# Three 512-column score units per key tile in six shared PSUM banks, and projections issued as 64-column pairs

## The chip, the cores and the metric

The kernel runs on one core of a Trainium2 chip. The metric is the device time of one execution in microseconds (us). Engines are named as the profile names them: PE is TensorE's matrix multiply, PEld its weight load, DVE is VectorE, ACT is ScalarE, POOL is GpSimd, SP is SyncE, which here only issues DMAs. PSUM is the memory that PE writes; it has eight banks, each of 512 float32 columns over 128 partitions.

## The reference

Two stages follow each other. First a routed attention over 4 batches and 8 heads, 768 positions, head size 64: a query sees only the keys whose nearest centroid (16 a head) is its own. Then a gated long convolution over the positions, with the attention's output as input (512 channels).

```python
q_assign = np.argmax(np.einsum('bhsd,hcd->bhsc', q_n, c_n), axis=-1)
k_assign = np.argmax(np.einsum('bhsd,hcd->bhsc', k_n, c_n), axis=-1)
mask = q_assign[:, :, :, None] == k_assign[:, :, None, :]
scores = np.where(mask, scale * np.matmul(q, k.transpose(0, 1, 3, 2)), -1000000000.0)
attn = softmax(scores)            # over the keys
x = np.matmul(attn, v)            # heads side by side: (4, 768, 512)
...
x1, x2, x3 = split(x @ w_proj)    # three times 512 columns
x2_conv = irfft(rfft(x2, axis=1) * rfft(filter_fft, axis=0), axis=1)
out = (x1 * x2_conv * x3) @ w_out
```

## The kernel before

Nothing is looped at run time. `build` writes down a list of operations, each with the engines that can do it, an estimated duration, a due time and what it reads and writes; `Plan.place` then puts them one by one on the engine that can start one first, among those about equally early the one with the earliest due time. The sequence that comes out is emitted as the program, so each engine runs a fixed list in order and waits where a needed result is late.

The attention works in 8 groups `n` of four heads (half a batch), each in two pairs `pr` of heads; a pair has six key tiles `sk` of 128 keys, so there are 96 key tiles. The operations that the change and the prediction speak of, with the lines of the kernel before:

- `tr` (L474): transposes of q and k, three 128x128 float32 transposes to one PSUM bank, copied out to `qkT` (L230 on ACT, L232 on DVE) and cast to `aug` (bfloat16, with 16 rows of one-hot cluster marks, `ohT`, below or above them, which makes the mask part of the product).
- `sim` (L494), `simT` (L505), `ohT` (L531): products with the centroids, their transposes, and the transposes of the one-hot marks; between them DVE finds the maxima (L509 to L521).
- `score` (L56, through `columns`): for one key tile and one head, four matmuls with 64 weight columns each into a pair of PSUM banks, 2 x 384 queries; `columns` issues two such matmuls, one for each half of the output's partitions, in the place of one with 128 weight columns.
- `exp` (L564): ACT reads the pair of banks (128 x 768) and writes the probabilities to `p`, of which there are four buffers (`NPB`), each for a key tile of both heads.
- `pv` (L575): the product with v for both heads, four float32 matmuls (each runs as two passes, so eight rows in the trace), accumulated over the six key tiles in banks 4 and 5; `acc` (L586) sums the probabilities on DVE; `den` (L599) adds them over the partitions.
- the convolution of a batch, spread between later attention work: `U` (L688), `spectrum` (L388, L392), `G` (L733), `I` (L758), `W` (L780). All but L392 are issued with 128 weight columns. The filter's own spectrum is computed once near the start with the same `spectrum`, from `filter_fft`, which DVE first adds and subtracts to `uv2` (L362).

PE is set to a tile shape by each matmul: 128 weight columns (projections, transposes), 64 (`score`, `pv`, `columns`), or 32 (`sim`, `den`), on 128 rows, and 64 rows x 128 columns for half of `I`. Two matmuls with 64 columns on different halves run beside each other. The planner charges 0.1 us for a change of shape (`switch`).

PSUM before: banks 0 to 3 are two pairs for scores alone, 4 and 5 the accumulator of `pv`, and 6 and 7 take everything else ("fill"); `banks_for` decides this. Before the first and after the last score the reserved banks are open to others too.

Queues: SP issues the loads of q, k, v, of `filter_fft` and the masks' rows; POOL's queue issues the loads of `w_proj` (`wpj`, needed first by `U`) and `w_out`.

Of the kernel before, what the change touches and what calls it, by code (L numbers as in the profile page):

```python
# [30 lines left out]
NPB = 4  # L31
# [3 lines left out]
MODES = {"pv": 64, "score": 64, "bc": 64, "sim": 32, "den": 32}  # L35
# [24 lines left out]
class Plan:  # L60
# [33 lines left out]
    def place(self, free0, banks_for, switch=0.1, wait=0.1, rate=215e3, bonus=4.0):  # L94
# [4 lines left out]
        st = SimpleNamespace(pool=0.0, dve=0.0, bw=0.0, last=None, kind=None, score=0, o=0, tail=0)  # L99
# [13 lines left out]
        while n < len(self.ops):  # L113
            best = None
            for e, lst in ready.items():
# [14 lines left out]
                if not cand:  # L130
# [3 lines left out]
                    c[1].due - (bonus if e == "PE" and st.kind == "pv" == c[1].kind else 0.0)  # L134
                    + (c[0] - t0) * 20, c[1].seq))
# [5 lines left out]
            if o.alloc is not None:  # L141
# [5 lines left out]
                if o.alloc.cls not in ("score", "o"):  # L147
                    st.tail |= (st.score == st.scores and min(o.alloc.ids) < 4) + 2 * (
                        st.o == st.otiles and any(i in (4, 5) for i in o.alloc.ids))
            d = o.eng[e]  # L150
            if e == "PE":
                mode = MODES.get(o.kind, 128)
                if mode != st.last:
                    d += switch
                st.last, st.kind = mode, o.kind
            o.start, o.on = t, e
            free[e] = t + d
            busy[e] += d
            o.end = t + d
# [8 lines left out]
            for h in o.free:  # L168
                h.readers -= 1
                h.end = max(h.end, o.end)  # L170
                if not h.readers:
                    for i in h.ids:
                        bank_free[i] = h.end + 0.06
# [12 lines left out]
def banks_for(bank, free, st, o):  # L186
# [5 lines left out]
    if bank.cls == "score":  # L192
        two = min(((0, 1), (2, 3)), key=lambda p: max(free[p[0]], free[p[1]]))
        t = max(free[two[0]], free[two[1]]) if st.score else whole(0, 4)
        return (two, t) if t < 1e8 else None
# [3 lines left out]
    allowed, first = [6, 7], []  # L199
    if st.score == 0:  # L200
        allowed += [0, 1, 2, 3] if bank.cls == "head" else []
    elif st.score == st.scores:
        if st.tail & 1:
            allowed += [0, 1, 2, 3]
        elif whole(0, 4) < 1e8:
            first += [0, 1, 2, 3]
    if st.o == 0:
        allowed += [4, 5] if bank.cls == "head" else []
    elif st.o == st.otiles:
        if st.tail & 2:  # L210
            allowed += [4, 5]
        elif whole(4, 6) < 1e8:
            first += [4, 5]
    t = lambda i: whole(*((0, 4) if i < 4 else (4, 6))) if i in first else free[i]
# [4 lines left out]
def build(T):  # L219
# [14 lines left out]
    columns = lambda *a: halves(T.nc.tensor)(*a)  # L234
# [10 lines left out]
    def two(h):  # L245
        return T.pair[h.ids[0] // 2]
# [770 lines left out]
```

## Time and profile before

| | before |
|---|---|
| median of 3 runs | 443.53 us (443.04 to 444.03) |
| the profiled execution | 443.23 us |
| its span, first to last instruction | 441.4 us |
| PE busy | 409.6 us, 93% |
| DVE busy | 355.5 us, 81% |
| ACT busy | 268.8 us, 61% |
| POOL busy | 96.0 us, 22% |
| granted PE clock, mean | 0.994 |

A busy PE is not a measure of its work here: the end of a matmul is modelled and lies behind the start of the next one. What an operation holds PE for is read from the start of its first matmul to the start of the next operation's first one.

### The profile page before, as it was taken

To read this page: it belongs to the slowest core of one execution; us is meant where nothing else is said; L and a number is where in the kernel's file an instruction comes from. 1 tells how busy PE (TensorE), PEld (TensorE's weight loads), DVE (VectorE), ACT (ScalarE), POOL (GpSimd) and SP (SyncE) were. 2 spreads that over 40 slices of the span, in tenths; PEclk is the share of its full clock that TensorE was granted. 3 is DMA by queue.
4 is the path that set the end of the run, shared out by engine and by line. 5 is a ranking of instruction groups with operands and counts; after the bars stand their busy time and mean duration, and the time that the engine had idled before them with its cause. 6 is when DMAs were issued, how large, how long until landed. Compare 5 with 4: busy or idle time off the path is not lost.

```text
span 441.4 us, 7484 instructions
## 1 busy us (share of the span) xinstructions
PE 409.6 (93%) x2824; PEld 189.8 (43%) x2840; DVE 355.5 (81%) x486; ACT 268.8 (61%) x411; POOL 96.0 (22%) x94
## 2 busy tenths in 40 slices
PE   4987698999999999999999999998999989999994
PEld 3444244444444444343434444443443434444541
DVE  7984999799897978687768977998956987887962
ACT  5885356688675566566574676757674455655242
POOL 6420000002102762111100541302300531220330
PEclk9999899999999999999999999999999999999999
DMA  9969806244421133112561114211140100111023
GB/s 198 169 128 251 182 20 146 73 107 97 106 74 49 43 74 93 53 47 81 193 135 36 55 38 107 73 44 48 61 156 5 52 1 1 38 38 50 1 95 143
DMA packets 67356, 37.11 MB, mean 84 GB/s; under 512 B 56764, under 2 KB 62456, under 8 KB 67320
## 3 DMA queue, kind: packets, MB, share of 16 engines
q1 hardware_dynamic: 62856, 33.62, 29.0%
q0 software_dynamic: 1056, 2.10, 2.7%
q10 hardware_dynamic: 3408, 0.92, 1.1%
q8 instruction: 22, 0.36, 0.3%
q14 instruction: 14, 0.11, 0.1%
HBM read 30.66 MB, written 6.48 MB: 84 GB/s over the span
## 4 chain that ended last, share of the span: by engine, by line
PE 66%; DVE 15%; DMA 7%; ACT 5%; issue 4%; SPq 1%; POOL 1%; ACTq 1%; DVEq 0%; POOLq 0%
PE pair L575 19%; PE pair L56 10%; PE bank L733 10%; DVE acc L586 6%; PE bank L688 5%; PE bank L780 5%; PE bank L758 4%; DMA y<-in_moe_filter_fft_dram 4%; PE bank L474 3%; PE bank L388 3%; PE bank L599 2%; DVE osb L648 2%; ACT p L564 2%; DVE uT L659 2%; PE bank L494 2%
## 5 line engine op out<-in xcount | busy, mean ns | idle before, releaser
L564 ACT ACTIVATE p<-pair 128x768 f32<-128x768 f32 x192 | 148.2, 811 | 65.8 <-PE pair L56 51.3
L575 PE MATMUL pair<-p,vraw 128*64 128x385 f32 x768 | 140.1, 493 | 0.9 <-ACT osb L591 0.9
L586 DVE TENSOR_TENSOR acc<-acc,p 128x1536 f32<-128x1536 f32 x64 | 116.7, 1823 | 5.9 <-ACT p L564 3.9
L56 PE MATMUL pair<-aug,aug 80*64 80x384 bf16 (+1 forms) x768 | 88.1, 334 | 6.9 <-ACT p L564 6.5
L575 PEld LDWEIGHTS pair<-p,vraw 128*64 128x64 f32 x768 | 56.1, 137 | 52.2 <-issue 43.1
L56 PEld LDWEIGHTS <-aug 80*64 80x64 bf16 (+1 forms) x768 | 37.9, 109 | 54.6 <-issue 46.1
L710 POOL TENSOR_TENSOR y<-tm 128x512 bf16<-128x512 f32 x21 | 36.1, 1729 | 113.0 <-DVE tm L706 84.3
L733 PE MATMUL bank<-xT,wpj 128*128 128x384 bf16 x256 | 48.2, 327 | 0.4 <-ACT qkT L230 0.4
L768 POOL TENSOR_TENSOR y<-yy,x 128x768 bf16<-128x768 f32 x12 | 25.2, 2100 | 98.4 <-DVE yy L764 73.2
L232 POOL CAST aug<-qkT 64x768 bf16<-64x768 f32 x18 | 20.6, 1144 | 112.8 <-ACT qkT L230 105.3
L474 PE MATMUL bank<-ident,qkraw 128*128 128x128 f32 x192 | 34.1, 301 | 8.3 <-DMA qkraw<-in_q_dram 5.2
L733 PEld LDWEIGHTS <-wpj 128*128 128x128 bf16 x256 | 22.5, 98 | 26.9 <-issue 14.9
L474 PEld LDWEIGHTS bank<-ident,qkraw 128*128 128x128 f32 x192 | 22.5, 149 | 24.8 <-issue 6.5
L230 ACT COPY qkT<-bank 128x384 f32<-128x384 f32 x50 | 23.0, 484 | 16.1 <-PE bank L733 8.8
L706 DVE TENSOR_TENSOR tm<-bank,hm 128x512 f32<-128x512 f32 x48 | 30.2, 681 | 2.0 <-PE bank L388 1.9
L586 DVE TENSOR_TENSOR acc<-p,p 128x1536 f32<-128x1536 f32 x16 | 28.5, 1781 | 3.2 <-PE bank L599 2.6
L688 PE MATMUL bank<-wpj,uT 128*128 128x512 bf16 x91 | 22.3, 380 | 0.9 <-DVE den L232 0.5
L780 PE MATMUL bank<-wout,y 128*128 128x512 bf16 x90 | 21.9, 380 | 0.4 <-POOL y L768 0.2
L232 DVE COPY qkT<-bank 128x384 f32<-128x384 f32 x22 | 12.1, 552 | 11.5 <-PE bank L474 11.2
L742 DVE TENSOR_TENSOR x<-bank,x 128x384 f32<-128x384 f32 x24 | 13.3, 552 | 9.6 <-PE bank L733 9.2
L230 ACT CAST aug<-qkT 64x768 bf16<-64x768 f32 x24 | 19.9, 829 | 0.8 <-DVE qkT L232 0.4
L758 PE MATMUL bank<-inv,y 128*128 128x384 bf16 (+1 forms) x128 | 20.0, 328 | 0.0
(136 smaller groups left out, 394.3 us busy)
## 6 DMA issues: line engine op xcount, KB each, us to landing
vraw<-in_v_dram SPq DMA_DIRECT2D x16, 384.0 KB
qkraw<-in_q_dram SPq DMA_DIRECT2D x30, 192.0 KB
qkraw<-in_k_dram SPq DMA_DIRECT2D x30, 192.0 KB
rb<-dr SPq DMA_DIRECT2D x30, 192.0 KB
out_dram<-ob SPq DMA_DIRECT2D x11, 512.0 KB
wpj<-in_moe_w_proj_dram POOLq DMA_DIRECT2D x1, 1536.0 KB, 13.6
y<-in_moe_filter_fft_dram SPq DMA_DIRECT2D x4, 384.0 KB
aug<-ohT SPq DMA_DIRECT2D x60, 24.0 KB
```

Source lines behind the costliest of these rows:

```text
L56: tensor.matmul(out[64 * i:64 * i + 64], lhsT[:, 64 * i:64 * i + 64], rhs, start=start, stop=stop)
L230: T.nc.scalar.copy(out, in_)
L232: (T.nc.vector if e == "DVE" else T.nc.gpsimd).tensor_copy(out, in_)
L474: T.nc.tensor.transpose(ap(h)[:, ts(t, 128)], T.qkraw[s][:, 3 * ch + t].rearrange("p h d -> p (h d)"), T.ident)
L564: ex = op(("ACT", .82 + (1.28 if first[0] is None else 0)), lambda e, h=h, s=s, hp=hp: T.nc.scalar.activation(T.p[s][:, hp, :S].rearrange( ...
L575: T.nc.tensor.matmul(o[64 * hp:64 * hp + 64, ch, :385], T.vraw[vs][:, hp, sk * D:(sk + 1) * D], T.p[slots[sk]][:, hp, 384 * ch:384 * ch + ...
L586: T.nc.vector.tensor_tensor(T.acc[:], x, T.p[slots[sk]][:, :, :S], op=Alu.add)
L688: T.nc.tensor.matmul(ap(h), f[:, e_, kt, ts(m, 128)], T.wpj[:, kt, DM:2 * DM], start=(kt == 0), stop=(kt == ND - 1))
L710: op(({"POOL": 1.45, "DVE": .68} if i < 2 else {"DVE": .68}) if last else ("POOL", 1.45), lambda e, i=i, r=r: alu(e).tensor_tensor(T.y[:, ...
L733: T.nc.tensor.matmul(ap(h)[:, :384], T.wpj[:, kt, off + dt * 128:off + dt * 128 + 128], T.xT[xs][:, kt, ts(ch, 384)], start=(kt == 0), sto ...
L758: T.nc.tensor.matmul(bk(hh, e_)[:, :384], T.y[lo:hi, i, cs, ts(dt, 128)], T.inv[lo:hi, row], start=(n == 0), stop=(n == 3))
L780: T.nc.tensor.matmul(ap(h), T.y2[:, kt, ts(2 * tt + e_, 128)], T.wout[:, kt], start=(kt == 0), stop=(kt == ND - 1))
```

## The change

**Banks.** Banks 0 to 3, 6 and 7 become six single banks for scores and fill alike. While scores are running, `banks_for` gives neither class more than `HELD` = 4 of them. Only 4 and 5 keep their special role.

**Scores.** The two heads' scores of a key tile, 2 x 768 columns, are cut into three units of 512 columns, each in one bank (`THIRDS`): 512 of the first head, 256 of each, 512 of the second. A unit is one `score` operation and one `exp`, so a key tile has three of each, where it had two. The middle unit has four pairs' halves of 256 columns.

**Shapes.** `U`, `spectrum`, `G`, `W`, the transposes `ohT` and half of `I` go through `columns` (or its like): two matmuls with 64 weight columns in the place of one with 128. The float32 transposes `tr`, `simT` stay at 128 columns, `sim` and `den` at 32. From the third group on, the transposes of both halves of a q or k tile (`tr2`, six of them, two banks) are one operation, and so are both halves of `sim` and of `simT`.

**Planner.** `place` adds 1.5 us (`shape`) to the due time of a PE operation that would change the shape, counts 0.16 us from PE's end to a result (`AFTER`), and 0.09 and 0.08 us of overlap on ACT and DVE (`OVERLAP`).

**Small things.** Three DVE operations on the one-hot marks are issued once for both halves (128 x 768) where there were two each. POOL copies one element of the filter's buffer into `wpj` ahead of the load of `w_proj`, so this load starts only after `filter_fft` has landed; the load of `w_out` stands ahead of it.

On PE, where the first convolution's `G` begins to mix with the attention (`bank` numbers are buffers, `pair` is the score's two banks, `wpj` the weights of `G`, `aug` those of the score). Before:

```order
L733 LDWEIGHTS wpj
L733 MATMUL bank_64<-xT_136,wpj 128x384
L599 MATMUL bank_63<-acc,ones_67 32x384 x4
L474 MATMUL bank_64<-ident,qkraw_87 128x128 x3
L56 LDWEIGHTS aug_103
L56 MATMUL pair_438<-aug_102,aug_103 64x384
```

The same place in the changed program, where L62 is `columns`, L476 `tr2` and L597 `pv`:

```order
L62 LDWEIGHTS aug_109
L62 MATMUL bank_65<-aug_108,aug_109 64x512
L597 MATMUL pair_492<-p_117,vraw_97 64x385 x4
L476 MATMUL bank_63<-ident,qkraw_91 128x128 x3
L476 MATMUL bank_66<-ident,qkraw_91 128x128 x3
L62 LDWEIGHTS wpj
L62 MATMUL bank_67<-xT_140,wpj 64x384
```

Before, the output's first number tells four shapes in six rows (128, 32, 128, 64 columns), three changes; now score, `pv` and `G` all have 64, and the two changes that are left stand around six transposes. Over the whole program the shape changes 284 times before and 134 times now.

On DVE, near the start, where the filter's `uv` (L362, now L363) stands among the first pair's sums `acc` (L586, now L608). Before:

```order
L516 TENSOR_TENSOR oh<-oh,revc 128x384
L519 TENSOR_REDUCE m_86<-oh 128x24
L521 TENSOR_TENSOR oh<-oh,m_86 128x384
L586 TENSOR_TENSOR acc<-acc,p_112 128x1536
L362 TENSOR_TENSOR uv_139<-y,y_141 128x1536 x2
L586 TENSOR_TENSOR acc<-acc,p_113 128x1536
L586 TENSOR_TENSOR acc<-acc,p_110 128x1536
```

Now:

```order
L608 TENSOR_TENSOR acc<-p_114,p_115 128x1536
L608 TENSOR_TENSOR acc<-acc,p_116 128x1536
L608 TENSOR_TENSOR acc<-acc,p_117 128x1536
L233 COPY sim<-bank_66 128x384
L608 TENSOR_TENSOR acc<-acc,p_114 128x1536
L608 TENSOR_TENSOR acc<-acc,p_115 128x1536
L363 TENSOR_TENSOR uv_143<-y,y_145 128x1536 x2
```

All five sums of the first pair now stand ahead of `uv`, of which two did before.

The diff, cut to what the text speaks of:

```diff
-MODES = {"pv": 64, "score": 64, "bc": 64, "sim": 32, "den": 32}
+HELD = 4
+THIRDS = [[(0, 0, 512)], [(0, 512, 768), (1, 0, 256)], [(1, 256, 768)]]
+HOLD = {"score": "score", "o": "o"}
+AFTER = {"PE": .16}
+OVERLAP = {"ACT": .09, "DVE": .08}
+MODES = {"pv": (64, 64), "score": (64, 64), "bc": (64, 64), "proj": (64, 64), "inv": (64, 65), "sim": (32, 32),
+         "den": (32, 32)}
...
                     c[1].due - (bonus if e == "PE" and st.kind == "pv" == c[1].kind else 0.0)
+                    + (shape if e == "PE" and MODES.get(c[1].kind, (128, 128))[0] != st.last else 0.0)
...
-    if bank.cls == "score":
-        two = min(((0, 1), (2, 3)), key=lambda p: max(free[p[0]], free[p[1]]))
...
-    allowed, first = [6, 7], []
+    allowed, first = [0, 1, 2, 3, 6, 7], []
+    if st.score and st.score < st.scores:
+        if st.held["score" if bank.cls == "score" else "fill"] + bank.n > HELD:
+            return None
...
     def spectrum(ps, i, cs):
-                T.nc.tensor.matmul(ps, T.fw[:, i, m, 192 * cs:192 * cs + 128], T.uv2[:, i, m],
-                                   start=(m == 0), stop=(m == 2))
+                columns(ps, T.fw[:, i, m, 192 * cs:192 * cs + 128], T.uv2[:, i, m], m == 0, m == 2)
...
-            for hp in range(2):
-                h = Bank("score", 2)
...
-                    for ch in range(2):
-                        columns(two(h)[:, ch, :384], ag[1][:K, ts(sk, 128)], ag[0][:K, ts(ch, 384)], True, True)
...
-                ex = op(("ACT", .82 + ...), lambda e, h=h, s=s, hp=hp: T.nc.scalar.activation(
-                    T.p[s][:, hp, :S].rearrange("p (a b) -> p a b", a=2), two(h)[:, :, :384], Act.Exp, scale=0.125),
+            for u in range(3):
+                h = Bank("score")
+                def sc(e, u=u, sk=sk, h=h):
+                    c = 0
+                    for hp, lo, hi in THIRDS[u]:
+                        K = 80 if hp == 0 else 128
+                        ag = T.augs[aset][pr][hp]
+                        columns(ap(h)[:, c:c + hi - lo], ag[1][:K, ts(sk, 128)], ag[0][:K, lo:hi], True, True)
+                        c += hi - lo
...
+                def exp(e, u=u, s=s, h=h):
+                    if u == 1:
+                        o = flat(s)[:, 512:1032].rearrange("p (a b) -> p a b", b=260)[:, :, :256]
+                        T.nc.scalar.activation(o, ap(h).rearrange("p (a b) -> p a b", a=2), Act.Exp, scale=0.125)
+                    else:
+                        lo = 0 if u == 0 else S + 4 + 256
+                        T.nc.scalar.activation(flat(s)[:, lo:lo + 512], ap(h), Act.Exp, scale=0.125)
...
                     def G(e, dt=dt, ch=ch, off=off, h=h):
-                            T.nc.tensor.matmul(ap(h)[:, :384], T.wpj[:, kt, off + dt * 128:off + dt * 128 + 128],
-                                               T.xT[xs][:, kt, ts(ch, 384)], start=(kt == 0), stop=(kt == ND - 1))
+                            columns(ap(h)[:, :384], T.wpj[:, kt, off + dt * 128:off + dt * 128 + 128],
+                                    T.xT[xs][:, kt, ts(ch, 384)], kt == 0, kt == ND - 1)
...
     def weights():
+        op(("POOL", .1), lambda e: T.nc.gpsimd.tensor_copy(T.wpj[0:1, 0, 0:1], T.f[1][0:1, 0, 0:1]), 39,
+           r=[("f", a, b) for a in range(2) for b in range(2)], w=["wpj"])
```

223 lines of the change are left out of this document (109 added, 114 removed).

## The prediction

> **What bounds the kernel now.** I read the page's engine line first, then the busy time by stage, then the waits. The stages are cut at the first `pv`, at the 24th, and at the last.
>
> ```profile
> span 441.4 us, 7484 instructions
> PE 409.6 (93%) x2824; PEld 189.8 (43%) x2840; DVE 355.5 (81%) x486; ACT 268.8 (61%) x411; POOL 96.0 (22%) x94
> ...
> PE 66%; DVE 15%; DMA 7%; ACT 5%; issue 4%; SPq 1%; POOL 1%; ACTq 1%; DVEq 0%; POOLq 0%
> ...
> 31.40:106.80 75.40, 66.30 (x491) 32.99 (x490) 63.43 (x79) 46.87 (x69) 0.83 (x1) 0.98 0.54 124
> 106.80:396.10 289.30, 281.05 (x1960) 124.75 (x1967) 234.90 (x302) 182.73 (x274) 70.66 (x41) 1.00 0.25 67
> 396.10:441.40 45.30, 39.11 (x233) 19.02 (x234) 30.75 (x48) 16.00 (x30) 9.08 (x6) 0.98 0.18 70
> ```
>
> The third row is the chain that ended last, by engine. The columns of the last three rows are length, then PE, PEld, DVE, ACT and POOL busy, the granted clock, DMA share and GB/s. In the long middle stage PE is busy 281.05 of 289.30 us (97%), DVE 81%, ACT 63%: there PE sets the pace. In the first stage PE has 88% and DVE 84%: neither alone does. The chain agrees: 66% of it is PE, 15% DVE.
>
> A busy PE still hides something, which only the starts show. The rows give start, length with the modelled end, and operation:
>
> ```profile
> 263.65 0.82 PE L733 MATMUL bank<-xT,wpj 128*128 128x384 bf16 x4
> 264.31 0.49 PE L474 MATMUL bank<-ident,qkraw 128*128 128x128 f32 x3
> 264.73 0.52 PE L56 MATMUL pair<-aug,aug 80*64 80x384 bf16 x4
> 265.19 1.46 PE L733 MATMUL bank<-xT,wpj 128*128 128x384 bf16 x8
> 266.58 0.52 PE L56 MATMUL pair<-aug,aug 128*64 128x384 bf16 x4
> 267.03 0.55 PE L474 MATMUL bank<-ident,qkraw 128*128 128x128 f32 x3
> 267.50 1.52 PE L575 MATMUL pair<-p,vraw 128*64 128x385 f32 x8
> 268.95 1.25 PE L758 MATMUL bank<-inv,y 128*128 128x384 bf16 x8
> ...
> 271.49 0.82 PE L56 MATMUL pair<-aug,aug 80*64 80x384 bf16 x8
> 272.14 1.46 PE L575 MATMUL pair<-p,vraw 128*64 128x385 f32 x8
> ...
> 322.00 1.46 PE L575 MATMUL pair<-p,vraw 128*64 128x385 f32 x8
> 323.29 0.82 PE L56 MATMUL pair<-aug,aug 80*64 80x384 bf16 x8
> ```
>
> None of them waited, and the shape is the number behind the star. A `pv` between two 64-column operations holds PE from 322.00 to 323.29, 1.29 us; between two others from 267.50 to 268.95, 1.45: its two changes cost 0.16. Two scores without a change take 0.65 (271.49 to 272.14), 0.33 each; one between others 0.46 (264.73 to 265.19): 0.13. Eight `G` matmuls between scores take 1.39 (265.19 to 266.58), against 1.30 for eight at the 0.163 us of a score's pair: 0.09. So leaving for a projection and coming back costs 0.09 + 0.13 = 0.22 between scores, 0.09 + 0.16 = 0.25 between `pv`s, and one change 0.117 us on the mean of both. None of it shows as idle time: the next start falls inside the modelled length of the one before.
>
> **The change part by part.**
>
> *Shapes and paired transposes.* Counted in the two orders, PE changes shape 284 times before and 134 times after: 150 fewer, 150 x 0.117 = 17.6 us of PE time. By stage (first `pv` to the 24th, and so on, as above): before the first `pv` and in the first stage 27 fewer (3.2 us), in the middle 117 fewer (13.7 us), behind the last `pv` 3 fewer (0.35 us). In the middle stage PE is the pace, so I count the 13.7 in full, and the 0.35.
>
> *Projections as pairs.* 572 matmuls become 1,144 with as many loads. What a pair costs is in the trace already:
>
> ```profile
> 59.63 0.84 PE L392 MATMUL bank<-uv,fw 128*64 128x512 bf16 x6
> 60.28 0.35 PE L56 MATMUL pair<-aug,aug 128*64 128x384 bf16 x2
> ...
> 327.80 1.04 PE L688 MATMUL bank<-wpj,uT 128*128 128x512 bf16 x4
> 328.67 0.49 PE L474 MATMUL bank<-ident,qkraw 128*128 128x128 f32 x3
> ```
>
> Three pairs of 512 columns in 64-column shape take 0.65 us, 0.217 each; four full-width ones take 0.87, 0.218 each. At 384 columns the score's pair has 0.163 and `G` 0.165 (263.65 to 264.31). Change: 0. The six `ohT` become twelve in pairs on the same ground: 0.
>
> *Score units.* Columns are unchanged, 1,536 a key tile. The outer units have a pair of 512 (0.217 each), the middle one two pairs of 256, which no row shows. The bounds: in proportion to the 384 pair 0.109, or no cheaper than that pair, 0.163. The nearest row is `20.57 ... x6` below: six 128-column transposes in pairs, whose starts end 0.36 - 0.22 = 0.14 us after the first, 0.056 a pair, so short pairs keep in proportion.
>
> ```profile
> 20.57 0.36 PE L355 MATMUL bank<-identb,fw 128*64 128x128 bf16 x6
> ...
> L355 PE MATMUL bank<-identb,fw 128*64 128x128 bf16 x12 | 0.7, 222 | 0.5 <-ACT inv L230 0.5
> ```
>
> I take 0.109: 0.217 x 2 + 0.109 x 2 = 0.65 a key tile, as the 2 x 0.33 of now. Upper end: 192 pairs x 0.054 = 10.4 us.
>
> *Exponentials.* Three of 512 columns for two of 768:
>
> ```profile
> L564 ACT ACTIVATE p<-pair 128x768 f32<-128x768 f32 x192 | 148.2, 811 | 65.8 <-PE pair L56 51.3 <-DVE acc L586 7.8 <-DVE uv L362 5.5
> ...
> L230 ACT CAST uv<-bank 128x512 bf16<-128x512 f32 x22 | 12.8, 587 | 6.6 <-PE bank L688 6.6
> ...
> L591 ACT COPY osb<-pair 128x770 f32<-128x770 f32 x16 | 12.8, 802 | 11.1 <-PE pair L575 10.9
> ...
> PE pair L56 <- ACT p L564: 6.5, 15, 1.0
> ```
>
> The last row is of the waits: in total, times, longest. A copy of 770 columns costs ACT the same as the exponential of 768 within 2% (802 against 811 ns), so I take the 587 ns of a copy of 512: 3 x 0.587 - 2 x 0.811 = 0.14 a key tile, 96 x 0.14 = 13 us more on ACT. Lower end 0; upper end 3 x 0.811, 78 us, which would make ACT 347. With 282 of some 425 us ACT has room, so 0 on the path. The cover is its own idle time of 51.3 us behind PE's scores; if it goes, `pv` waits for the third exponential. That wait replaces one on PE that six banks may end: PE stood 6.5 us for ACT to free a score pair.
>
> *One-hot operations.* 42 on DVE become 21 of double width:
>
> ```profile
> L521 DVE TENSOR_TENSOR oh<-oh,m 128x384 bf16<-128x384 bf16 x14 | 7.8, 556 | 0.4
> ...
> L519 DVE TENSOR_REDUCE m<-oh 128x24 bf16<-128x384 bf16 x14 | 7.7, 552 | 0.4
> ...
> L516 DVE TENSOR_TENSOR oh<-oh,revc 128x384 bf16<-128x384 bf16 x14 | 4.7, 338 | 0.0
> ```
>
> At most half of their 20 us goes, at least nothing. ACT's 811 ns for 768 and 587 for 512 leave a fixed part of 0.14 us an operation; if DVE's is like it, 21 x 0.14 = 3 us of DVE go. DVE isn't the pace: 0.
>
> *The start.* `wpj` now waits for the filter and `uv` stands behind five `acc`. Now:
>
> ```profile
> 44.64 3.42 DVE L362 TENSOR_TENSOR uv<-y,y 128x1536 bf16<-128x1536 f32 x2 [6.38 <-DMA y<-in_moe_filter_fft_dram]
> ...
> 46.45 0.81 PE L388 MATMUL bank<-uv,fw 128*128 128x512 bf16 x2 [3.46 <-DVE uv L362]
> ...
> 48.08 1.51 ACT L564 ACTIVATE p<-pair 128x768 f32<-128x768 f32 x2 [5.48 <-DVE uv L362]
> ...
> 52.97 0.81 PE L388 MATMUL bank<-uv,fw 128*128 128x512 bf16 x3 [1.32 <-DVE yy L375]
> ```
>
> DVE stood 6.38 us for the filter, PE 3.46 + 1.32. Both go if the filter lands before about 43, since it then shares the queues with less. Against that, the new order puts 16 score units ahead of the first `pv`; with six banks the 16th waits for the tenth exponential, some 10 x 0.587 = 5.9 us, while PE has 16 x 0.22 = 3.5 us to do: over 2 us of idle PE. And DVE, 84% busy in this stage, has nearly the same work to do. So of the 3.2 + 4.8 us I take half, 4; ends 0 and 8. POOL's queue, which stands with the waiting copy, has only a cast for the third group behind it; `U` wants `wpj` first near 130.
>
> *Tighter engines.* With the middle stage 13.7 shorter DVE is at 85% there. I add 1 us of new waits (0 to 5).
>
> Sum: 13.7 + 0.35 + 4 - 1 = 17 us off the span of 441.4: 424.4. The profiled execution had 443.23, 1.8 outside its span, so 426.2; the median of the runs is 0.3 above the profiled one: 426.5.
>
> **A rule that speaks against it.** The loads' rows first:
>
> ```profile
> L733 PEld LDWEIGHTS <-wpj 128*128 128x128 bf16 x256 | 22.5, 98 | 26.9 <-issue 14.9
> ...
> L56 PEld LDWEIGHTS <-aug 128*64 128x64 bf16 x384 | 19.8, 110 | 21.6 <-issue 16.3
> ```
>
> The Trainium skill ("TensorEngine Tiling (Array Packing)", section "Restrictions and Gotchas") says that column tiling rules out Fast Weight Load. The trace agrees so far that half a weight's load, 110 ns, takes no less than a whole one's, 98.
>
> **The rivals.**
>
> *DVE takes over.* It is within 2 us of full in some stretches of 20:
>
> ```profile
> 240.00:260.00 20.00, 19.24 (x141) 9.03 (x138) 18.58 (x23) 12.75 (x19) 10.25 (x6) 1.00 0.11 32
> ...
> 320.00:340.00 20.00, 19.89 (x132) 7.95 (x133) 11.43 (x19) 12.40 (x19) 0.00 (x0) 1.00 0.23 88
> 340.00:360.00 20.00, 17.93 (x128) 8.75 (x127) 18.67 (x25) 9.90 (x15) 9.43 (x6) 1.00 0.11 31
> ```
>
> If a third of the middle stage stays as long as DVE makes it, 4.6 of the 13.7 are lost, and the 4 at the start: 426.5 + 8.6 = 435. Against it: the row between has 11.43, so the work can move. Chance 0.22.
>
> *The waits go too.* PE's 6.5 us for score banks vanish by most, and the start gives 8: 426.5 - 4 - 4 = 418.5. For it: of six banks four may hold scores, cut finer. Chance 0.20.
>
> *Loads bound the pairs.* If two half loads follow each other at 0.110, a pair lasts no less than 0.22: 256 `G` and 64 `I` matmuls of 384 columns lengthen by 0.055, 17.6 us, and the gain is gone: 444, no change. Against it stand the scores, whose pairs run at 0.163 with loads of the same form. Chance 0.03.
>
> *Slower: `pv` waits for its third exponential.* A unit's exponential starts only when ACT is through with the two before; if each of 96 `pv`s stood 0.3 us for it, 29 us, the time would be 455. It decides from 17 / 96 = 0.18 us a key tile on. Against it: four `p` buffers let scores run ahead, and ACT is idle a third of the time. Chance 0.05.
>
> **How the numbers follow.** The forecast itself, 423 to 431 by the ends of the start and of the new waits, has 0.50. With the first two rivals the range is 418 to 437; it leaves out 0.08 and the outer part of those two, and takes in the 10.4 of the 256-column pairs. A change under 0.2%, 0.9 us, is about what a measurement of this kernel can't tell from none. Faster is the forecast and both of the first rivals: 0.92; same 0.02; slower 0.06.
>
> **What would show it.** Right: eight `G` matmul pairs between two scores last 1.30, no longer 1.39; PE's busy time falls by some 15 us with the same columns; exponentials of 512 near 0.59 us; no wait of DVE for the filter. Wrong: pairs of 384 over 0.17 or of 256 over 0.13 from start to start; PE waiting for exponentials by more than some 10 us; DVE over 90% busy in the middle stage, with PE waiting for `acc`, `tm` or `uT`.

## The result, and the profile after

The changed kernel takes 415.38 us (median of 4, 414.99 to 416.50) where the one before takes 443.49 (443.04 to 444.03): a ratio of 0.937, 95% interval 0.9349 to 0.9391. That is 28 us, where 17 were forecast, and below the range's lower end of 418. The profiled execution took 415.38, its span 413.6. Times here and below are medians of the executions in the fast state; two stand outside it, 433.39 us of after_noest and 1368.8 of after_tr_single.

First the page's engine line and the chain by engine, then the three stages (cut as before at the first, the 24th and the last `pv`), with the columns of the prediction's stage rows:

```profile
span 413.6 us, 8836 instructions
...
PE 388.7 (94%) x3454; PEld 212.3 (51%) x3454; DVE 355.0 (86%) x460; ACT 279.4 (68%) x522; POOL 87.2 (21%) x84
...
PE 62%; DVE 23%; ACT 7%; issue 5%; DMA 1%; ACTq 1%; POOL 0%; DVEq 0%
```

```profile
34.10:95.80 61.70, 59.23 (x488) 31.72 (x490) 54.81 (x62) 43.65 (x82) 3.00 (x3) 1.00 0.63 138
95.80:369.40 273.60, 267.06 (x2414) 141.04 (x2413) 243.11 (x296) 193.48 (x361) 66.09 (x33) 1.00 0.28 74
369.40:413.60 44.20, 39.02 (x401) 24.19 (x398) 31.70 (x50) 16.52 (x30) 3.35 (x3) 0.98 0.19 73
```

The span lost 27.8 us: 11.0 up to the 24th `pv` (106.8 before, 95.8 now), 15.7 in the middle stage (289.3 to 273.6), 1.1 in the tail. PE is still the pace, at 98% in the middle, and DVE has come close: 243.11 of 273.6, 89%, and its share of the chain has grown from 15% to 23%.

The timeline of PE in the stretch with `G` (start, length with the modelled end, operation) answers to the prediction's first rows. Here the `G` matmuls are at L62 with `wpj`, the scores at L62 with `aug`:

```profile
151.29 1.46 PE L597 MATMUL pair<-p,vraw 128*64 128x385 f32 x8
152.59 0.82 PE L62 MATMUL bank<-xT,wpj 128*64 128x384 bf16 x8
153.33 0.87 PE L476 MATMUL bank<-ident,qkraw 128*128 128x128 f32 x6
154.14 0.84 PE L62 MATMUL bank<-xT,wpj 128*64 128x384 bf16 x8
154.81 0.82 PE L62 MATMUL bank<-aug,aug 80*64 80x512 bf16 x8
155.47 1.46 PE L597 MATMUL pair<-p,vraw 128*64 128x385 f32 x8
156.76 0.82 PE L62 MATMUL bank<-xT,wpj 128*64 128x384 bf16 x8
157.41 0.82 PE L62 MATMUL bank<-inv,y 128*64 128x384 bf16 x8
```

`pv` to `G` now takes 1.30 (151.29 to 152.59): no change of shape is paid. Four `G` pairs take 0.65 (156.76 to 157.41), 0.163 each. A change is still paid around the six transposes.

For the sections below I split PE's time of each kernel: its matmuls by the start-to-start durations of the prediction's rows, plus its changes of shape at their prices (0.117 us on the mean). I call this the bare work; what is left of a stage I call the rest. Before, the bare work is 396.6 us of the span, now 379.5: 17.1 less. The rest fell from 44.8 to 34.1, by 10.7, and most of what the prediction missed is in it.

The bare work is priced, not measured: its level is uncertain by some us (the expectation of before_shared below has 265.9 for the middle of the changed kernel, the table 268.0), and only differences carry. What the rows themselves show of PE's waiting is its idle time, length less busy time: in the middle stage 289.30 - 281.05 = 8.25 us before and 273.60 - 267.06 = 6.54 now, 1.7 less. The rest there fell by 4.6; the other 2.9 are short waits below the modelled ends or errors of the prices.

### The profile page after: what moved, and what is told of

It is laid out like the page before. It is cut to its first block, busy times and chain, and to the rows that moved or that the text cites. A ratio compares the mean times of both kernels' runs of the same rounds, so it can differ in the third digit from the quotient of the medians.

```text
span 413.6 us, 8836 instructions
## 1 busy us (share of the span) xinstructions
PE 388.7 (94%) x3454; PEld 212.3 (51%) x3454; DVE 355.0 (86%) x460; ACT 279.4 (68%) x522; POOL 87.2 (21%) x84
## 4 chain that ended last, share of the span: by engine, by line
PE 62%; DVE 23%; ACT 7%; issue 5%; DMA 1%; ACTq 1%; POOL 0%; DVEq 0%
PE bank L62 31%; PE pair L597 17%; DVE acc L608 12%; DVE tm L728 4%; PE bank L621 3%; PE bank L504 2%; ACT p L587 2%; PE bank L476 2%; DVE uT L681 2%; DVE osb L670 2%; PE bank L781 1%; DMA qkraw<-in_k_dram 1%; PE bank L486 1%; PE bank L517 1%; ACT qkT L231 1%
## 5 line engine op out<-in xcount | busy, mean ns | idle before, releaser
L597 PE MATMUL pair<-p,vraw 128*64 128x385 f32 x768 | 142.7, 488 | 1.5 <-ACT qkT L231 0.9
L587 ACT ACTIVATE p<-bank 128x512 f32<-128x512 f32 x192 | 113.8, 610 | 41.1 <-PE bank L62 35.8
L608 DVE TENSOR_TENSOR acc<-acc,p 128x1536 f32<-128x1536 f32 x64 | 122.7, 1918 | 9.7 <-ACT p L587 7.8
L62 PE MATMUL bank<-aug,aug 80*64 80x512 bf16 (+3 forms) x768 | 90.5, 328 | 2.3 <-ACT p L587 0.4
L597 PEld LDWEIGHTS pair<-p,vraw 128*64 128x64 f32 x768 | 55.6, 136 | 49.2 <-issue 39.4
L62 PEld LDWEIGHTS <-aug 80*64 80x64 bf16 (+1 forms) x768 | 43.3, 109 | 40.2 <-issue 28.4
L584 ACT ACTIVATE p<-bank 128x512 f32<-128x512 f32 x96 | 58.4, 608 | 4.5 <-PE bank L62 4.3
L62 PE MATMUL bank<-xT,wpj 128*64 128x384 bf16 x512 | 51.4, 327 | 0.2 <-ACT p L587 0.2
L62 PEld LDWEIGHTS <-wpj 128*64 128x64 bf16 x512 | 29.2, 109 | 19.1 <-issue 9.3
L608 DVE TENSOR_TENSOR acc<-p,p 128x1536 f32<-128x1536 f32 x16 | 28.1, 1754 | 11.8 <-ACT p L587 10.7
L62 PEld LDWEIGHTS <-y 128*64 128x64 bf16 x320 | 18.5, 110 | 14.8 <-issue 4.4
L62 PE MATMUL bank<-wout,y 128*64 128x512 bf16 x192 | 22.5, 379 | 0.0
L62 PE MATMUL bank<-wpj,uT 128*64 128x512 bf16 x192 | 22.1, 379 | 0.0
L476 PEld LDWEIGHTS bank<-ident,qkraw 128*128 128x128 f32 x144 | 15.3, 140 | 10.7 <-issue 5.3
L476 PE MATMUL bank<-ident,qkraw 128*128 128x128 f32 x144 | 20.8, 281 | 0.0
L621 PE MATMUL bank<-acc,ones 128*32 128x384 f32 x128 | 13.6, 496 | 7.0 <-DVE acc L608 5.5
L681 DVE TENSOR_TENSOR uT<-osb 128x384 bf16<-128x384 f32 x32 | 19.1, 630 | 0.5
## 6 DMA issues: line engine op xcount, KB each, us to landing
wpj<-in_moe_w_proj_dram POOLq DMA_DIRECT2D x1, 1536.0 KB, 13.7
```

The costliest lines, as they stand in the source:

```text
L62: tensor.matmul(out[64 * i:64 * i + 64], lhsT[:, 64 * i:64 * i + 64], rhs, start=start, stop=stop)
L476: T.nc.tensor.transpose(bank(h.ids[i // 3])[:, ts(i % 3, 128)], raw(s, i), T.ident)
L584: T.nc.scalar.activation(o, ap(h).rearrange("p (a b) -> p a b", a=2), Act.Exp, scale=0.125)
L587: T.nc.scalar.activation(flat(s)[:, lo:lo + 512], ap(h), Act.Exp, scale=0.125)
L597: T.nc.tensor.matmul(o[64 * hp:64 * hp + 64, ch, :385], T.vraw[vs][:, hp, sk * D:(sk + 1) * D], T.p[slots[sk]][:, hp, 384 * ch:384 * ch + ...
L608: T.nc.vector.tensor_tensor(T.acc[:], x, T.p[slots[sk]][:, :, :S], op=Alu.add)
```

## The experiments

### A ladder from the kernel before to the changed one

Each rung adds a part. Times are medians of 4 runs; the stages are those of each kernel's profiled execution.

| kernel | median us | to 24th `pv` | middle | its bare work | its rest | tail | shape changes |
|---|---|---|---|---|---|---|---|
| before | 443.5 | 106.8 | 289.3 | 279.1 | 10.2 | 45.4 | 284 |
| before_gate | 437.21 | 100.5 | 289.9 | 279.1 | 10.8 | 45.4 | 284 |
| before_planned_gate_noest | 431.79 | 100.3 | 280.7 | 269.2 | 11.5 | 50.3 | 173 |
| before_planned_gate | 426.37 | 100.3 | 280.6 | 271.6 | 9.0 | 44.2 | 176 |
| after_ownbanks_single | 423.82 | 96.3 | 278.0 | 272.6 | 5.4 | 44.7 | 176 |
| after_allsingle | 418.08 | 96.3 | 275.8 | 269.9 | 5.9 | 44.2 | 162 |
| after | 415.38 | 95.8 | 273.6 | 268.0 | 5.6 | 44.2 | 134 |

**POOL's copy alone** (before_gate). The order of the other engines stays as it was before; on POOL's queue the load of `w_out` now stands ahead of that of `w_proj`.

```diff
     def weights():
+        op(("POOL", .1), lambda e: T.nc.gpsimd.tensor_copy(T.wpj[0:1, 0, 0:1], T.f[1][0:1, 0, 0:1]), 39,
+           r=[("f", a, b) for a in range(2) for b in range(2)], w=["wpj"])
```

> The kernel before with only POOL's copy added ahead of the load of the projection weights (planner run again). Theory 'the filter': the wait of DVE for it, 6.4 us, and of PE for uv, 3.5 us, go, and the time falls by 4 to 9 us, to 435 to 439. Rival 'order and banks': by less than 3 us.

Measured: 437.21, ratio 0.9848 (0.9823 to 0.9874): 6.8 us less. In the profiled executions the stages up to the 24th `pv` are 6.3 shorter and the others no shorter. The prediction knew 3.46 + 1.32 = 4.8 us of idle PE. The windows of the kernel before, around that wait, show the rest:

```profile
44.00:46.00 2.00, 0.00 (x0) 0.00 (x0) 1.36 (x1) 0.00 (x0) 0.00 (x0) 1.00 1.17 293
46.00:48.00 2.00, 1.49 (x8) 0.73 (x10) 2.00 (x3) 0.00 (x0) 0.00 (x0) 0.80 1.29 222
48.00:50.00 2.00, 2.00 (x12) 0.95 (x10) 1.90 (x3) 1.51 (x2) 0.00 (x0) 0.50 0.78 169
50.00:52.00 2.00, 1.65 (x12) 0.62 (x9) 2.00 (x2) 0.95 (x2) 0.00 (x0) 0.84 0.65 144
52.00:54.00 2.00, 1.03 (x5) 0.39 (x6) 2.00 (x3) 1.27 (x2) 0.00 (x0) 1.00 0.65 197
```

```profile
48.47 2.53 PE L575 MATMUL pair<-p,vraw 128*64 128x385 f32 x8
```

After the idle stretch the granted clock (third column from the end) goes down to 0.50, and a `pv` of 1.46 lasts 2.53. By these clocks some 2 x (0.20 + 0.50 + 0.16) = 1.7 us more are lost, an estimate; with the 4.8 that makes 6.5 of the 6.8. The Trainium skill ("TensorE: Matmul & The Clock Gate", section "Part 1: The HAM clock gate") says that about 3.4 us of idling halve TensorE's clock; the trace agrees, with 3.46 us of idling and 0.50. With the copy, the same place in before_gate, windows and then DVE:

```profile
44.00:54.00 10.00, 9.47 (x70) 4.33 (x68) 9.34 (x14) 5.53 (x8) 0.00 (x0) 1.00 1.02 218
```

```profile
38.36 3.43 DVE L362 TENSOR_TENSOR uv<-y,y 128x1536 bf16<-128x1536 f32 x2 [0.39 <-DMA y<-in_moe_filter_fft_dram]
```

The filter's product starts at 38.36 instead of 44.64, after a wait of 0.39 instead of 6.38, and the clock stays at 1.00.

**The same copy taken out of the changed kernel** (after_nogate): the two lines above removed.

> The changed kernel without POOL's copy ahead of the load of the projection weights, so this load again runs beside the filter's (the planner is run again; 140 changes of shape). Theory 'the 7 us missed at the start are the filter': 5 us or more over 415.4, DVE waiting again for the filter. Rival 'the start is shorter by the order and the banks, the filter is hidden behind the five sums': within 2 us of 415.4.

Measured: 418.40, 0.9425 (0.9407 to 0.9443), 3.0 over the changed kernel. The expected wait did not return: the planner, run again, starts `uv` at 58.81 instead of 42.58, behind ten sums instead of five, and DVE has no wait for the filter at all. So the 3.0 are the price of an order that makes room for a late filter, with 6 more changes of shape in it (6 x 0.117 = 0.7).

**Pairs and the planner's price for a shape, old units and banks** (before_planned_gate_noest). The projections go through `columns`, `place` has the `shape` term and the new `MODES`; scores stay 768 wide in two bank pairs. Against before_gate:

```diff
-    def place(self, free0, banks_for, switch=0.1, wait=0.1, rate=215e3, bonus=4.0):
+    def place(self, free0, banks_for, switch=0.1, wait=0.1, rate=215e3, bonus=4.0, shape=1.5):
...
+                    + (shape if e == "PE" and MODES.get(c[1].kind, (128, 128))[0] != st.last else 0.0)
...
+                            columns(ap(h)[:, :384], T.wpj[:, kt, off + dt * 128:off + dt * 128 + 128],
+                                    T.xT[xs][:, kt, ts(ch, 384)], kt == 0, kt == ND - 1)
```

> before_planned_gate without the planner's 0.16 us behind PE and the overlaps on ACT and DVE; 173 changes of shape, 3 fewer. Theory 'the estimates take waits out of the order': 431 to 437. Rival 'it is the shapes alone': 425 to 428.

Measured: 431.79, 0.9728 (0.9703 to 0.9754), 5.4 below before_gate. By the table it is two things: the middle stage's bare work falls by 9.9, but the tail grows from 45.4 to 50.3.

**With the estimates** (before_planned_gate): the lines that were left out, now in.

```diff
+AFTER = {"PE": .16}
+OVERLAP = {"ACT": .09, "DVE": .08}
...
+            free[e] = t + d - OVERLAP.get(e, 0.0)
+            o.end = t + d + AFTER.get(e, 0.0)
```

> The kernel before with the pairs, the planner's new terms (1.5 us against a change of shape, 0.16 us behind PE, overlap on ACT and DVE) and POOL's copy, but with the old score units of 768, the old banks and the old transposes. 176 changes of shape. Theory 'shapes, order and filter make the gain': 437.2 with the copy alone, less 108 changes at 0.078 to 0.117 us, so 425 to 429, and less again if the planner's order has fewer waits. Rival 'units and banks carry what is left': no lower than 425. At 418 or less units and banks are worth nothing.

Measured: 426.37, 0.9620 (0.9599 to 0.9640), another 5.4, and 6.1 in the tail alone. In the middle they add 2.4 of bare work and take 2.5 of the rest, but PE's idle time there does not fall (7.2 without them, 7.6 with them), so fewer waits in the middle are not shown. The tail is plain: without the estimates PE stands 2.13 us ahead of `den` for the last sum, and the granted clock is 0.50 from 385.2 to 392.1 us, which at half speed is up to 3.4 us more; with them it stays at 1.00 there.

**The changed kernel without the estimates** (after_noest): `AFTER = {}` and `OVERLAP = {}`.

> The changed kernel without the planner's 0.16 us behind PE and the overlaps on ACT and DVE (140 changes of shape). Theory 'the better estimates took the waits out': 419 or more. Rival 'estimates hardly matter': within 2 us of 415.4.

Measured: 427.81 (426.40 to 431.97), 0.9674 (0.9614 to 0.9734), 12.4 over the changed kernel in the median. The profiled execution, the fastest, is 11.0 over it: 6.3 of this in the tail (50.5), 2.0 in the middle, 2.6 ahead of it. In the tail PE again stands ahead of `den`, 2.55 us, and the granted clock is 0.50 from 378.9 to 385.7. In the changed kernel products with `wout` stand at that place (370.74 to 372.56) and the clock stays at 1.00. Both orders show that the estimates mostly mend the tail. (The idle stretches ahead of these two drops of the clock, 2.13 and 2.55 us, are shorter than the 3.46 above.)

**Units of 512 in single banks of their own** (after_ownbanks_single): the changed kernel, but scores in banks 0 to 3 alone and all else in 6 and 7; transposes, `sim` and `simT` one operation per half.

```diff
+    if bank.cls == "score":
+        allowed = [0, 1, 2, 3]
+    elif st.score and st.score < st.scores:
+        allowed = [6, 7]
...
-            if n > 1 and ch == 0:
+            if False:
...
-        h = Bank(cls, 2)
+        for ch in range(2):
+            h = Bank(cls)
```

> The changed kernel with units of 512 in banks 0 to 3 alone and all else in 6 and 7 while scores run, and with the transposes, sim and simT in single-bank operations as before, so that none of them needs both fill banks. 180 changes of shape. Theory 'sharing the banks is the rest': 422 to 428, near before_planned_gate (426.4). Rival 'finer units': 416 to 420. If it stays near 445, units of 512 are worse than the old ones in banks of their own.

Measured: 423.82 (420.76 to 425.05), 0.9541 (0.9499 to 0.9583). Up to the 24th `pv` the time falls by 4.0 and the middle's rest by 3.6 (PE's idle time from 7.6 to 3.5), with 176 changes of shape, as many as before. The 4.0 are not the units' alone: in before_planned_gate the granted clock is 0.50 from 17.6 to 24.4 and from 31.2 to 38.1 us, here from 20.3 to 23.7 only, and 10.3 us less at half clock could be worth all of them. The profiled execution was the fastest of the four, so the table's row flatters this rung by some 3 us, and how the gain splits between it and the next is open by as much.

**Shared banks** (after_allsingle): the edit above without the four added lines of its first piece.

> The changed kernel with the transposes, sim and simT in single-bank operations, shared banks kept. 162 changes of shape, 28 more: 2 to 3 us more than 415.4. It tells what of the 30 us between after_ownbanks and the changed kernel was the two-bank operations. Rival 'pairs cost waits': no more than 415.4, as after_tr_single.

Measured: 418.08, 0.9426 (0.9404 to 0.9448): 5.7 less by the medians, 2.7 by the spans of the two profiles. Bare work in the middle falls by 2.7, changes of shape from 176 to 162: with more banks to choose from, the planner strings equal shapes together. PE's idle time in the middle is back at 7.5, nearly all of it ahead of `den`. Pairing the operations of two halves, the last rung, gives 2.7 more (162 to 134 changes, 28 x 0.117 = 3.3).

### What a change of shape costs

**The projections full width again, in the changed order** (after_wide). Not one instruction's place changes, only pairs become single 128-column matmuls.

```diff
-                            columns(ap(h)[:, :384], T.wpj[:, kt, off + dt * 128:off + dt * 128 + 128],
+                            wide(ap(h)[:, :384], T.wpj[:, kt, off + dt * 128:off + dt * 128 + 128],
```

(and so for `U`, `spectrum`, `W`, `ohT`, the first half of `I`; `wide` is one plain matmul)

> The changed kernel with its order of operations untouched, but U, spectrum, G, W, ohT and the first half of I issued as one matmul with 128 weight columns each. PE changes shape 264 times instead of 134. Theory 'a change of shape costs 0.117 us wherever PE is the pace': 130 x 0.117 = 15.2 us more than 415.4, so 430 to 431. Rival 'the shapes are worth more than their starts show' (they would explain the 11 us that the prediction missed): 436 or more. Rival 'the shapes are cheap, the banks did it': under 424.

Measured: 425.56, 0.9590 (0.9563 to 0.9617): 10.2 more for 130 more changes, 0.078 each and not 0.117. The price is there in full where PE doesn't wait. `spectrum` (`uv,fw`) between scores in the changed kernel's timeline of PE:

```profile
127.37 0.82 PE L62 MATMUL bank<-uv,fw 128*64 128x512 bf16 x6
128.01 0.39 PE L62 MATMUL bank<-aug,aug 128*64 128x512 bf16 x2
128.23 0.82 PE L62 MATMUL bank<-uv,fw 128*64 128x512 bf16 x6
128.88 0.61 PE L62 MATMUL bank<-aug,aug 80*64 80x512 bf16 x6
129.32 0.82 PE L62 MATMUL bank<-uv,fw 128*64 128x512 bf16 x6
```

and the same place in after_wide, where the full-width matmuls are at L238:

```profile
129.94 0.82 PE L238 MATMUL bank<-uv,fw 128*128 128x512 bf16 x3
130.69 0.41 PE L62 MATMUL bank<-aug,aug 128*64 128x512 bf16 x2
131.03 0.82 PE L238 MATMUL bank<-uv,fw 128*128 128x512 bf16 x3
131.78 0.63 PE L62 MATMUL bank<-aug,aug 80*64 80x512 bf16 x6
132.34 0.82 PE L238 MATMUL bank<-uv,fw 128*128 128x512 bf16 x3
```

`spectrum` takes 0.75 (129.94 to 130.69) where it took 0.64, a unit with two changes about it 0.56 (131.78 to 132.34) where it took 0.44. In the middle stage the bare work is 281.6, 13.6 more, and the stage 9.2 longer: 4.4 us of the rest went, and PE's idle time there is 3.1 us instead of 6.5, since a slower PE stands less for the others. The reverse holds as well.

**Pairs in the old order** (before_pairs): the same edit the other way round, made to the kernel before: 84 changes of shape fewer, nothing moved.

> The kernel before with its order of operations untouched, but the same projections issued as pairs of 64-column matmuls. 200 changes of shape instead of 284. Theory '0.117 us a change': 84 x 0.117 = 9.8 us less than 443.5, so about 434, if none of it turns into waits. Rival 'more than the starts show': 427 or less. Rival 'other engines take the gain': over 438.

Measured: 438.59, 0.9896 (0.9863 to 0.9929): 5.4 less than the 444.0 beside it, where 84 x 0.117 is 9.8. The profiled execution is the slowest of the four (441.24; the others 438.45 to 438.69), with the granted clock at 0.50 for 10.2 us between start and end; in the kernel before it is for 3.4. In it the bare work of the middle fell by 7.5, the stage by 3.0. The waits of the score pairs, 6.5 in the kernel before, are now:

```profile
PE pair L56 <- ACT p L565: 7.4, 16, 1.1
```

So without other edits nearly half of the saved time is not paid out; how it splits between waits and the clock this one profile does not tell. That was the prediction's fear; in the changed kernel it did not come.

### Which part of the bank scheme counts

**Own banks, two-bank operations kept** (after_ownbanks): the changed kernel with only those four lines added.

> The changed kernel with its units of 512, but while scores run these get banks 0 to 3 alone and all else 6 and 7, as before (planner run again, 150 changes of shape). Theory 'shared banks end PE's waits': 422 or more, with PE waiting for the exponentials by some 6 us again. Rival 'the finer units do it alone': 416.5 to 418, the 16 changes.

Measured: 445.67, 1.0059 (1.0031 to 1.0086): 30 more than the changed kernel. With operations of one bank each (after_ownbanks_single), 22 of the 30 go. A paired operation needs both of the two fill banks at once, which would explain it. Part is the clock again: in the middle stage, 27 us longer than in the changed kernel, it is 0.50 for 13.6 us, up to 6.8 us of the loss. PE's waits in after_ownbanks are many and spread out; the longest on banks are for readers of one of them:

```profile
PE bank L62 <- DVE x L768: 4.0, 4, 1.7
PE bank L62 <- ACT p L591: 3.6, 3, 2.6
PE bank L548 <- DVE tm L732: 3.0, 1, 3.0
```

**Transposes unpaired** (after_tr_single): `if n > 1 and ch == 0:` becomes `if False:`, so that transposes go in threes; `sim` and `simT` stay paired.

> The changed kernel with the transposes of q and k in threes again, one bank each, for all groups (planner run again, 150 changes of shape, 16 more). By 0.078 to 0.117 us a change: 416.6 to 417.3. Rival 'the pairs of transposes need two free banks at once and cost waits': no more than 415.4.

Measured: 415.03 (414.60 to 415.54), 0.9360 (0.9341 to 0.9379), with 150 changes of shape: no difference. The 2.7 of the last rung come from `sim` and `simT`, or from these together with the transposes.

**Old units of 768 with shared banks** (before_shared): before_planned_gate with score pairs from three bank pairs and fill work from all six, each pair of banks declared as one two-bank tile.

```diff
+        two = min(((0, 1), (2, 3), (6, 7)), key=lambda p: max(free[p[0]], free[p[1]]))
...
+    allowed, first = [0, 1, 2, 3, 6, 7], []
...
-        return T.bank[i][:]
+        return T.pair[i // 2][:, i % 2]
```

> As before_planned_gate, with the old score units of 768 columns in a pair of banks, but three pairs (banks 0 to 3, 6 and 7) shared by scores and fill, four banks at most for either. 160 changes of shape instead of 176, PE's bare work in the middle stage 265.9 us, as in the changed kernel. Theory 'sharing the banks is the rest': 415 to 419. Rival 'the finer units are the rest': 422 or more, with PE waiting for exponentials.

Measured: 454.95, 1.0241 (1.0202 to 1.0280), 29 more than before_planned_gate. This was to price the unit's size apart from sharing, and the next run shows that it can't.

**Two-bank tiles in the changed kernel** (after_pairtiles): same plan, same banks, same instructions; only the declaration of the banks is that of before_shared (its last two lines of diff).

> The changed kernel with the same plan, the same banks and the same instructions, but each two neighbouring banks declared as one tile, as before_shared had to have them. If waits are kept by bank: 415.4. If operations on one bank of a tile also wait for those on the other, it is slower by much (430 or more), and before_shared's 455 is due to that and says nothing on sharing.

Measured: 454.23, 1.0224 (1.0200 to 1.0247): 39 more. An operation on one bank now waits for the readers of its neighbour too. The waits that the changed kernel (0.7 us on the first of these) has not:

```profile
PE pair L62 <- ACT p L587: 7.9, 15, 1.0
...
PE pair L62 <- DVE yy L787: 2.4, 5, 0.9
PE pair L62 <- ACT x L231: 2.1, 5, 0.6
```

So waits are kept by declared tile, not by bank, and sharing pays only with each bank declared by itself: otherwise it costs more than the whole change gains. before_shared has the same declaration and so says nothing on the unit's size.

**Four units of 384** (after_quarters):

```diff
-THIRDS = [[(0, 0, 512)], [(0, 512, 768), (1, 0, 256)], [(1, 256, 768)]]
+THIRDS = [[(0, 0, 384)], [(0, 384, 768)], [(1, 0, 384)], [(1, 384, 768)]]
```

> The changed kernel with four units of 384 columns a key tile in the place of three of 512, each in a shared bank (137 changes of shape, PE's bare work the same). ACT has four exponentials of some 0.49 us for three of 0.61, 12 us more in all. Theory 'single shared banks, the size does not matter': 415 to 419. Rival 'the size of 512 fills the banks, at most four of them for scores': 425 or more, PE waiting for exponentials.

Measured: 415.78, 0.9365 (0.9351 to 0.9379): the same. ACT is busy 284.8 us where it was 279.4, and that costs nothing. Between 384 and 512 columns the unit's size does not matter as long as a unit has one bank.

**No limit on the banks of one class** (after_held6): `HELD = 6`.

> The changed kernel without the limit of four of the six banks for scores or for fill (136 changes of shape). If the limit keeps one class from starving the other: 418 or more. If not: 413 to 417, and then it may be the fastest.

Measured: 419.93, 0.9451 (0.9417 to 0.9485), 4.5 more, 3.7 of it in the middle stage (277.3).

### Is DVE the next bound?

**The sums' last use later** (after_den_later). PE's longest wait in the changed kernel is `den` (L621) for the sum:

```profile
DVE acc L608 <- ACT p L587: 18.5, 10, 3.3
...
PE bank L621 <- DVE acc L608: 5.5, 6, 1.1
```

```diff
-        op(("PE", .68), den, te + .5, r=["acc", "ones"], w=[h], alloc=h, kind="den")
+        op(("PE", .68), den, te + (.5 if last else 3.0), r=["acc", "ones"], w=[h], alloc=h, kind="den")
```

> The changed kernel with the product den due 2.5 us later in the planner, since PE's largest wait is now for acc ahead of den, 5.5 us in 6 waits. If those waits are PE's alone: 410 to 413. If DVE is the pace at these places, PE only waits elsewhere: within 1.5 us of 415.4.

Measured: 418.44, 0.9424 (0.9402 to 0.9445): 3.0 more. The wait fell as meant, to 2.3, and others came for it:

```profile
PE bank L62 <- ACT p L584: 2.7, 1, 2.7
PE bank L621 <- DVE acc L608: 2.3, 2, 1.6
```

DVE is close, but it waits itself 18.5 us for exponentials ahead of its sums; no run shows it as the bound.

## Why the prediction was wrong, and where it was right

**Shapes: right as work.** Projected were 13.7 + 0.35 + 3.2 = 17.3 us of PE time, found 17.1 of bare work (11.1 in the middle stage, 5.6 ahead of it, 0.4 behind). PE's busy time fell by 20.9, where "some 15" stood. (The prediction's 27 changes up to the 24th `pv` are 30 by the order: 27 + 117 + 3 is not 150. That makes its 3.2 a 3.5.) But "In the middle stage PE is the pace, so I count the 13.7 in full" would not have held by itself: before_pairs got 5.4 of 9.8, after_wide gave back 10.2 of 15.2. It is paid out in full only where the waits don't grow.

**"Tighter engines. ... I add 1 us of new waits": the wrong sign, the first step that failed.** PE's busy time in the middle stage fell by 14.0 us, where 13.7 were forecast; its idle time fell by 1.7, where 1 more was forecast. Together these are the 3.0 us by which this stage beat the forecast (15.7 for 12.7). A new wait did come: PE's wait of `den` for its sum is 5.5 us, 0.4 before. But the main sum put at nothing what the banks would save, and PE's waits for the exponentials to free a score bank, 6.5 us before, all but went:

```profile
PE bank L62 <- ACT p L587: 0.7, 2, 0.4
```

In the ladder this wait is 4.3 in before_planned_gate and 1.8 with single-bank units. How the fall of the rest splits between the estimates, the units and the sharing is not shown: the priced rest and PE's idle time go different ways from rung to rung.

**"The start": mis-sized, the second step that failed.** 4 was taken, 11.0 came off, which is 7.0 of the 10.8 that the prediction missed. The filter's wait was priced at PE's idle time of 4.8; taken away by itself it gives 6.8, since the clock falls after it. Then it was halved, together with the shapes, because "DVE, 84% busy in this stage, has nearly the same work to do": DVE's busy time in the first stage fell from 63.43 to 54.81, and rose in the middle from 234.90 to 243.11. Part of this is work that now stands in other stages, and part of the rise are the longer sums of the last section. And the step from old to new units, which the prediction counted only as a cost here, brings another 4.0 up to the 24th `pv`, in part by the clock.

The feared cost of the 16 units ahead of the first `pv` is not shown. The first `pv` is at 34.1, not 31.4, but before_planned_gate, with four scores of 768 columns ahead of it as before, has it at 33.3 already. PE stands 1.4 us between the first score and the first `pv`, 0.4 of it for an exponential. The prediction's count was off as well: with four banks at most for scores (`HELD`) the 16th unit waits for the 12th exponential, not for the tenth.

**Tail.** 0.35 forecast, 1.1 found. What the forecast did not see is that pairs and the rule on shapes by themselves make it 4.9 longer, and the estimates 6.1 shorter, by the wait ahead of `den` and the clock behind it.

**The range.** The ends of the two uncertain terms, 0 to 8 and 0 to 5, add up to 421.5 to 434.5, not to the 423 to 431 that the prediction gives its forecast; either way the time lies below.

**Pairs, units, exponentials: right within 4%.** A pair of 384 has 0.163. The 256-column pair, bounded by 0.109 and 0.163, has 0.11: the three pairs of two units take 0.44 (128.88 to 129.32), less 0.217, by two. The loads and exponentials, from the page's groups:

```profile
L587 ACT ACTIVATE p<-bank 128x512 f32<-128x512 f32 x192 | 113.8, 610 | 41.1 <-PE bank L62 35.8
...
L584 ACT ACTIVATE p<-bank 128x512 f32<-128x512 f32 x96 | 58.4, 608 | 4.5 <-PE bank L62 4.3
...
L62 PEld LDWEIGHTS <-wpj 128*64 128x64 bf16 x512 | 29.2, 109 | 19.1 <-issue 9.3
```

An exponential of 512 takes 610 ns, not 587, and ACT is busy 279.4 us where 282 was forecast. Their cover held: ACT still idles 35.8 us behind PE's scores.

**One-hot operations: right.** The groups of double width:

```profile
L533 DVE TENSOR_TENSOR oh<-oh,m 128x768 bf16<-128x768 bf16 x7 | 6.7, 955 | 0.2
L531 DVE TENSOR_REDUCE m<-oh 128x48 bf16<-128x768 bf16 x7 | 6.7, 951 | 0.2
L528 DVE TENSOR_TENSOR oh<-oh,revc 128x768 bf16<-128x768 bf16 x7 | 3.7, 529 | 0.1
```

17.1 us in place of 20.2: 3.1 less, 3 forecast. DVE's whole busy time stayed at 355, though, in part because the sums take 5.6 us longer (last section).

**The rivals.** "The waits go too" (418.5) was the nearest, and right in kind: PE's wait for score banks all but vanished and the start gave more than 8. It still lacked 3 us. "DVE takes over" (435) was half seen: 89% busy in the middle, 5.5 us of PE's waits, but no bound. "Loads bound the pairs" (444) is refuted: the pairs last 0.163 us with two half loads of 109 ns each, and 512 such loads keep PEld busy for 29.2 us, so they overlap. The Trainium skill ("TensorEngine Tiling (Array Packing)", section "Restrictions and Gotchas") says that column tiling rules out Fast Weight Load; in this trace that costs nothing. "`pv` waits for its third exponential" (455) does not show in the waits: PE stood for exponentials 0.7 us in all.

What stays open: how the 8.3 us between before_planned_gate and after_allsingle split between single-bank units and sharing, to within some 3 us; and whether part of the first is DVE's merged one-hot operations, or the banks that are open to more work before the first and after the last score, which no run took apart.

## What to carry to other kernels

Price a change of shape by starts, then ask who will wait if PE gets faster: the same edit without new room for waiting paid only half. Price a wait by the idle time and by the clock behind it, and a busy engine in one stage by whether its work can move to the next. And where a planner or a tile framework sets the order, what it believes (its estimates, the tiles it counts waits by) is part of the change: here it was worth as much as the instructions.

## What was not expected of the hardware

DVE's sums and POOL's products hold each other up. A sum `acc` of two SBUF inputs takes 1.75 us alone, up to 3.19 beside a product of POOL; POOL's `y` takes 1.81 alone, up to 3.27. In all, by line (ns least, median, most), the changed kernel:

```profile
L791 POOL TENSOR_TENSOR y<-yy,x x12: 1809/3180/3266, 152.7 to 367.0; 128x768 bf16<-128x768 f32 x12
```

and before:

```profile
L768 POOL TENSOR_TENSOR y<-yy,x x12: 1811/1816/3199, 169.7 to 396.0; 128x768 bf16<-128x768 f32 x12
```

The median went from 1.82 to 3.18 us: 7 of the 12 products now start while a sum runs, and 2 did before. The timeline of the changed kernel shows one such meeting, POOL and then DVE:

```profile
349.65 3.18 POOL L791 TENSOR_TENSOR y<-yy,x 128x768 bf16<-128x768 f32 x1 [3.00 <-PE bank L62]
```

```profile
349.40 1.75 DVE L608 TENSOR_TENSOR acc<-acc,p 128x1536 f32<-128x1536 f32 x1
...
352.00 2.45 DVE L608 TENSOR_TENSOR acc<-acc,p 128x1536 f32<-128x1536 f32 x1
```

The sum from 349.40 ends at 351.15 as if alone; the product ends 1.68 us later, at 352.83; the next sum ends 1.62 behind that, at 354.45. Each seems to have stood until the other was through. The Trainium skill ("SBUF — State Buffer", section "SBUF: two separate sides") says so: an exclusive lock between GpSimd and a VectorE operation with two SBUF inputs. The trace agrees; no run here took the meetings away. All sums `acc` together are busy 150.8 us now (122.7 + 28.1) and were busy 145.2 before (116.7 + 28.5).
